# Windowed attention with sink keys: each 128-row block's key band stored as two 64-row halves of 224 columns

## The chip, the cores and the metric

One core of a Trainium2 chip runs the kernel. The metric is the device time of one execution in microseconds (us); the time before is the median of three runs.

## What is computed

Attention with a sliding window of 128 keys and 4 sink keys, for 2 batches of 8 heads, 768 positions and head size 64, in float32. Its output, 768 x 512 for each batch, goes through two blocks of matrix products (a low-rank token mix and a channel network of width 2048; then a token network of width 256 and a channel network of width 1536). Only the attention is touched here:

```
keep   = (key < 4) | ((row - key >= 0) & (row - key < 128))
scores = where(keep, (q @ k.T) / 8, -1e9)
a      = softmax(scores);  out = a @ v
```

So a block of 128 rows needs its own 128 keys, the 128 keys before them, and the first few keys (the sinks). Both limits (4 and 128) are inputs; the masks leave room for up to 32 sinks.

## The kernel before

TensorE (PE) does all products, VectorE (DVE) takes scores out of PSUM, ScalarE (ACT) takes exponentials, GpSimd (POOL) does small steps, and SyncE (SP) issues every DMA. PE and SP run in the order in which the program writes them; the order on DVE, ACT and POOL is the compiler's.

**Attention** (`band_attention`, L296 to L351). The work is 16 units: a batch, a pair of heads, and a half of the rows (half 0 has the blocks i = 0, 1, 2; half 1 has i = 3, 4, 5). A unit has three steps, one for each block, so there are 48 steps t. A step passes three slots; after each slot the planner (`weave`) may put in side work.

- Slot 1, `band_scores` (L197): for each of the two heads e one product of the 64 x 128 queries with 288 columns: 128 keys before, 32 sinks, 128 own keys. Block 0 has only its own 128. Head 0 uses array rows 0 to 63 and head 1 rows 64 to 127; each writes a PSUM bank of its own (0 and 1). Then `band_soft`: DVE adds the mask and takes the minimum of the negated scores (L209), and ACT takes the exponential and the row sum (L213). The result `pr` is stored with the two heads alternating along the columns.
- Slot 2, two steps later, `band_turn`: PE transposes for each head the 128 columns before (L230) and the own 128 (L231; L233 in block 0), and once for both heads the sink columns (L238, from block 2 on). `band_keep` copies them out of PSUM (L247, on ACT for the first block of a unit, on DVE otherwise), and at the end of a unit copies the transposed sinks (L250).
- Slot 3, four steps later, `band_values` (L266): products with the values, in two parts; a block of values serves the own keys of one row block and the keys before of the next in one product of 256 columns, or 128 where there is only one of them. Each head writes 64 of the 128 output rows. Then one product for the sinks of both heads (L272), a copy out (L277), three transposes back (L282), and the division by the row sums (L289, L290).

**Loads.** SP loads a unit's queries and keys at once (`band_load`, L170: 384 query columns and 448 or 608 key columns, two units ahead), the values of a head pair in half 0 (L179), and the sink values (L180).

**Side work.** `weave` (L670) gives each slot a grant of time for PE, DVE, ACT and POOL (`SPREAD`: 0.3, 0.3, 0.3, 0.4 us while fewer than 8 units are finished, then 0.7, 0.6, 0.6, 0.7), adds it to what is left over (at most 1.5), and lets two side lists take steps whose costs are written at their `yield`. A `yield` with a fifth number holds its side for that many slots. The first list (`FEEDS`) decodes weights: `decode_steps` (L423) loads a piece of 512 float64 values for each partition, and turns them into two float32 parts by ACT and POOL (L434, L435), three steps on DVE (L437, L439, L441), and ACT and POOL again (L443, L444). The second (`FILLS`) has the token mix (`mix_down`, `mix_up`) and three "narrow" channel passes c0, c1, c2 (`channel_pass`: products `hp` at L124, ACT and DVE at L623 and L624, products `accs` at L643); c0 starts when the low-rank weights and four weight tiles are decoded. `drain` runs what is left when the attention has been written out.

**After the attention** (from about 188 us) the channel passes of full width run, PE products from end to end (`layers`).

Of the kernel before, what the change touches and what calls it, by code (L numbers as in the profile page):

```python
# [20 lines left out]
P = 128  # L21
# [6 lines left out]
KW = P + SINK  # L28
BAND = P + KW
K0 = 3 * P + 2 * SINK  # L30
K1 = 4 * P + 3 * SINK
MASKED = -8.0e9
FAR = 1.0e30
ATTENTION = {"sc": (0, 1), "tp": (3,), "tsink": (5,), "ot": (6,), "xp": (6,), "tall": (2,), "mix": (4, 7), "acc": (2, 7), "hid": (4,)}
# [8 lines left out]
CHUNK, HOLD = 4, 3  # L43
WARM = 3
# [31 lines left out]
class Net:  # L76
# [4 lines left out]
    def preload(self, x):  # L81
# [4 lines left out]
        n = HALF + K0  # L86
        self.early = flat[:, NS * P:NS * P + n]
        nc.sync.dma_start(self.early, self.ins["qk"][0, 0, 0, :, :n])
        self.ident = c.tile([P, P], F32, name="ident")
        make_identity(nc, self.ident)  # L90
        key, rel, self.span, self.sink = flat[:, :P], flat[:, P:2 * P], flat[:, 2 * P:2 * P + BAND], flat[:, 2 * P + BAND:3 * P + BAND]
        self.key = key
        nc.gpsimd.iota(rel, pattern=[[-1, P]], base=0, channel_multiplier=1, allow_small_or_imprecise_dtypes=True)
        nc.gpsimd.iota(key, pattern=[[1, P]], base=0, channel_multiplier=0, allow_small_or_imprecise_dtypes=True)
        nc.gpsimd.memset(self.span[:, P:KW], 0.0)
        nc.gpsimd.tensor_scalar(self.span[:, :P], rel, float(P), None, ALU.add)
        nc.gpsimd.tensor_scalar(self.span[:, KW:], rel, 0.0, FAR, ALU.is_lt, ALU.mult)
        nc.gpsimd.tensor_tensor(self.span[:, KW:], self.span[:, KW:], rel, ALU.add)
# [45 lines left out]
    def band_masks(self):  # L144
        nc, c = self.nc, self.one
        m0 = c.tile([P, P], F32, name="m0")
        m1 = c.tile([P, BAND], F32, name="m1")
        m2 = c.tile([P, BAND], F32, name="m2")

        def put(out, place, bound):  # L150
            nc.vector.tensor_scalar(out, place, bound, MASKED, ALU.is_ge, ALU.mult)

        put(self.sink, self.key, self.n_sink)
        put(m2, self.span, self.window)
        nc.vector.tensor_tensor(m0, m2[:, KW:], self.sink, ALU.max)
        nc.vector.tensor_tensor(m1[:, 0:P], m2[:, 0:P], self.sink, ALU.max)
        nc.vector.memset(m1[:, P:KW], MASKED)
        put(m1[:, KW:], self.span[:, KW:], self.window)
        put(m2[:, P:KW], self.key[:, 0:SINK], self.n_sink)
        self.masks = [m0, m1] + [m2] * (NS - 2)  # L160

    def band_load(self, unit, ld):
        nc = self.nc
        b, hp, half = unit
        nk = K1 if half else K0
        if unit == (0, 0, 0):
            raw = self.early
        else:
            raw = ld.tile([P, HALF + K1], F32, tag="qk", name="qk", bufs=3)
            nc.sync.dma_start(raw[:, :HALF + nk], self.ins["qk"][b, hp, half, :, :HALF + nk])  # L170
        return {"unit": unit, "raw": raw}

    def band_load_values(self, st, ld):
        nc = self.nc
        b, hp, half = st["unit"]
        if half == 0:
            self.v = ld.tile([P, NS, P], F32, tag="v", name="v")
            self.vs = ld.tile([P, 2 * D], F32, tag="vs", name="vs")
            nc.sync.dma_start(self.v, self.ins["v"][b, hp])  # L179
            nc.sync.dma_start(self.vs, self.ins["vs"][b, hp])  # L180
        st["v"], st["vs"] = self.v, self.vs
# [5 lines left out]
    def band_scores(self, st, ii):  # L187
        nc = self.nc
        half = st["unit"][2]
        i = 3 * half + ii  # L190
        n = BAND if i else P
        k0 = HALF + (ii if half else max(ii - 1, 0)) * KW
        st["sc", ii] = []
        for e in range(2):
            sc = self.bank("sc", "sc")[:, :n]
            head = st["raw"][e * D:(e + 1) * D]
            nc.tensor.matmul(sc, lhsT=head[:, blk(ii)], rhs=head[:, k0:k0 + n], start=True, stop=True)  # L197
            st["sc", ii].append(sc)

    def band_soft(self, st, ii, e, sb):  # L200
        nc = self.nc
        nb, den = st["nb"], st["den"]
        i = 3 * st["unit"][2] + ii
        n = BAND if i else P
        if e == 0:
            st["pr", ii] = sb.tile([P, BAND, 2], F32, tag="pr", name="pr", bufs=3)
        pr = st["pr", ii]
        sm = sb.tile([P, BAND], F32, tag="sm", name="sm", bufs=3)
        nc.vector.tensor_tensor_reduce(  # L209
            sm[:, :n], st["sc", ii][e], self.masks[i][:, :n], scale=-0.125, scalar=3.0e38,  # L210
            op0=ALU.add, op1=ALU.min, accum_out=nb[:, ii, e:e + 1],
        )
        nc.scalar.activation(  # L213
            pr[:, :n, e], sm[:, :n], AF.Exp, bias=nb[:, ii, e:e + 1], scale=-1.0,
            accum_out=den[:, ii, e:e + 1],
        )

    def band_turn(self, st, ii, e):
        nc = self.nc
        half = st["unit"][2]  # L220
        i = 3 * half + ii
        if ii == 0 and e == 0:
            st["pt"] = self.sb.tile([P, 2, 3 * 2 * P], F32, tag="pt", name="pt")
            st["pts"] = self.sb.tile([P, HALF], F32, tag="pts", name="pts")
        pr, pt = st["pr", ii], st["pt"]
        if e == 0:
            st["tp"] = self.bank("tp", "tp").rearrange("p (e k) -> p e k", e=2)
        tp = st["tp"]
        if i > 0:
            nc.tensor.transpose(tp[:, e, 0:P], pr[:, 0:P, e], self.ident)  # L230
            nc.tensor.transpose(tp[:, e, P:], pr[:, KW:, e], self.ident)  # L231
        else:
            nc.tensor.transpose(tp[:, e, P:], pr[:, 0:P, e], self.ident)  # L233
        first = 0 if half else 2
        if ii == first and e == 1:
            st["tsink"] = self.bank("tsink", "tsink")
        if i >= 2 and e == 1:
            nc.tensor.transpose(st["tsink"][:, blk(ii)], pr[:, P:P + D, :].rearrange("p s e -> p (s e)"), self.ident)  # L238

    def band_keep(self, st, ii):  # L240
        nc = self.nc
        half = st["unit"][2]
        pt, tp = st["pt"], st["tp"]
        first = 0 if half else 2
        lo = 0 if 3 * half + ii else P
        copy = nc.scalar.copy if ii == 0 else nc.vector.tensor_copy
        copy(pt[:, :, ii * 2 * P + lo:(ii + 1) * 2 * P], tp[:, :, lo:])  # L247
        if ii == 2:
            s0 = first * P
# [3 lines left out]
    def band_values(self, st, part):  # L253
        nc = self.nc
        half = st["unit"][2]
        pt, pts, v, vs = st["pt"], st["pts"], st["v"], st["vs"]
        if half == 0:
            sinks, steps = (2 * P, 1), [[(0, 0, 2, P)], [(1, P, 2, 3 * P), (2, 2 * P, 1, 5 * P)]]
        else:
            sinks, steps = (0, 3), [[(2, 0, 1, 0), (3, 0, 2, P)], [(4, P, 2, 3 * P), (5, 2 * P, 1, 5 * P)]]  # L260
        if part == 0:
            st["ot"] = self.bank("ot", "ot")
        ot = st["ot"]
        for n, (j, c0, w, p0) in enumerate(steps[part]):
            for e in range(2):
                nc.tensor.matmul(  # L266
                    ot[e * D:(e + 1) * D, c0:c0 + w * P], lhsT=v[:, j, e * D:(e + 1) * D], rhs=pt[:, e, p0:p0 + w * P],
# [635 lines left out]
```

## Time and profile before

| | us |
|---|---|
| median of 3 runs (672.05 to 675.17) | 673.8 |
| the profiled execution | 675.64 |
| its span, first to last instruction | 673.9 |
| PE busy | 655.1 |
| DVE busy | 380.1 |
| ACT busy | 233.1 |
| POOL busy | 187.7 |

"Busy" on PE counts products in flight, also while the next one waits for its weights or for the array to empty, so a busy PE is not PE at its peak. The granted clock is a share of full speed: 1.0 is 2.4 GHz and 0.5 is 1.2 GHz, the two levels that occur. The step times named below are starts of the first DVE step (L209) of a step t.

### The profile page before, as it was taken

Reading aid. Unit: us, or ns where it says so; the run is one execution under the profiler, and the core shown is the slowest. Engines: PE = TensorE matmul, PEld = TensorE weight load, DVE = VectorE, ACT = ScalarE, POOL = GpSimd, SP = SyncE. Lnnn points to the kernel's source line nnn. Section 1 sums busy time; section 2 is a strip of 40 time slices with the busy share of each in tenths; the row PEclk is TensorE's granted clock in tenths of the full one; section 3 lists DMA queues with packets and bytes.
Section 4 is the critical chain, followed back from the end, with each engine's and each line's share of the span. In section 5 each row is a group of like instructions: output and inputs, shape, how many; then the busy total and the mean of one; then the engine's idle time right before and its main releaser. Section 6 shows DMA issues by size and latency. Waiting matters only on the chain.

```text
span 673.9 us, 10189 instructions
## 1 busy us (share of the span) xinstructions
PE 655.1 (97%) x3958; PEld 601.1 (89%) x3958; DVE 380.1 (56%) x790; ACT 233.1 (35%) x568; POOL 187.7 (28%) x205
## 2 busy tenths in 40 slices
PE   8999998998999999999999999999999999999996
PEld 3565666786899999999999999999999999999996
DVE  4868794497354157888872345786241377422223
ACT  4756673355141133433321133532131243211110
POOL 1434562043010044544430022751040254200000
PEclk8999998998999999999999999999999999999999
DMA  4424541422000013434340010322000032000112
GB/s 138 146 80 147 208 146 54 147 100 94 1 1 0 1 46 112 139 116 127 130 146 1 1 63 8 119 94 94 1 1 0 1 125 95 2 0 1 48 48 98
DMA packets 16474, 48.53 MB, mean 72 GB/s; under 512 B 1952, under 2 KB 5152, under 8 KB 16416
## 3 DMA queue, kind: packets, MB, share of 16 engines
q1 hardware_dynamic: 16416, 47.79, 21.4%
q8 instruction: 33, 0.54, 0.3%
q14 instruction: 25, 0.20, 0.1%
HBM read 44.63 MB, written 3.15 MB: 71 GB/s over the span
## 4 chain that ended last, share of the span: by engine, by line
PE 88%; DVE 8%; issue 2%; ACT 1%; POOL 0%; DVEq 0%; ACTq 0%
PE hp L124 34%; PE accs L643 34%; PE sc L197 4%; PE gp L124 3%; PE ot L266 3%; PE up L124 2%; DVE c L439 1%; DVE sm L209 1%; PE tp L230 1%; PE tp L231 1%; DVE c L441 1%; DVE pt L247 1%; PE ot L272 1%; PE tp L124 1%; PE xtp L124 1%
## 5 line engine op out<-in xcount | busy, mean ns | idle before, releaser
L124 PE MATMUL hp<-uh,wh 128*128 128x384 f32 (+1 forms) x464 | 156.4, 337 | 6.1 <-DVE hl L624 6.1
L624 DVE SCALAR_TENSOR_TENSOR hl<-hp,hh 128x384 fp32r<-128x384 f32 (+1 forms) x116 | 62.8, 542 | 176.0 <-ACT hh L623 175.5
L124 PE MATMUL hp<-uh,wl 128*128 128x384 f32 (+1 forms) x464 | 154.1, 332 | 0.0
L643 PE MATMUL accs<-hh,wh 128*128 128x384 f32 (+1 forms) x464 | 154.1, 334 | 0.0
L124 PE MATMUL hp<-ul,wh 128*128 128x384 f32 (+1 forms) x464 | 153.9, 332 | 0.0
L643 PE MATMUL accs<-hh,wl 128*128 128x384 f32 (+1 forms) x464 | 151.9, 330 | 0.0
L623 ACT ACTIVATE hh<-hp 128x384 fp32r<-128x384 f32 (+1 forms) x116 | 55.6, 480 | 261.2 <-PE hp L124 261.1
L444 POOL TENSOR_TENSOR wl<-c,wh 128x512 fp32r<-128x512 f32 x56 | 75.7, 1355 | 172.3 <-ACT wh L443 170.0
L643 PE MATMUL accs<-hl,wh 128*128 128x384 f32 (+1 forms) x464 | 97.1, 329 | 0.0
L124 PEld LDWEIGHTS hp<-uh,wh 128*128 128x128 f32 x464 | 87.7, 189 | 9.9 <-DVE hl L624 6.8
L643 PEld LDWEIGHTS accs<-hh,wh 128*128 128x128 f32 x464 | 87.6, 189 | 2.7 <-ACT hh L623 1.5
L124 PEld LDWEIGHTS hp<-ul,wh 128*128 128x128 f32 x464 | 87.8, 189 | 0.1
L124 PEld LDWEIGHTS hp<-uh,wl 128*128 128x128 f32 x464 | 87.7, 189 | 0.0
L643 PEld LDWEIGHTS accs<-hh,wl 128*128 128x128 f32 x464 | 87.7, 189 | 0.0
L643 PEld LDWEIGHTS accs<-hl,wh 128*128 128x128 f32 x464 | 80.3, 188 | 0.0
L435 POOL TENSOR_SCALAR c<-c 128x512 f32<-128x512 f32 (+2 forms) x65 | 47.8, 735 | 77.4 <-ACT c L434 73.9
L651 DVE TENSOR_TENSOR x<-accs,x 128x384 f32<-128x384 f32 (+1 forms) x118 | 58.7, 557 | 16.8 <-PE accs L643 16.8
L213 ACT ACTIVATE pr<-sm,nb 128x288 f32<-128x288 f32 (+1 forms) x96 | 50.7, 533 | 43.1 <-DVE nb L209 42.5
L439 DVE SCALAR_TENSOR_TENSOR c<-raw,c 128x512 int32<-128x512 int32 (+2 forms) x65 | 60.2, 926 | 1.7
L434 ACT ACTIVATE c<-raw 128x512 f32<-128x512 f32 (+2 forms) x65 | 43.1, 664 | 34.0 <-POOL wl L444 23.8
L441 DVE SCALAR_TENSOR_TENSOR c<-raw,c 128x512 int32<-128x512 int32 (+2 forms) x65 | 53.0, 815 | 1.3
L437 DVE TENSOR_SCALAR c<-c 128x512 int32<-128x512 int32 (+2 forms) x65 | 43.4, 667 | 10.7 <-POOL c L435 10.7
(151 smaller groups left out, 752.0 us busy)
## 6 DMA issues: line engine op xcount, KB each, us to landing
raw<-in_w SPq DMA_DIRECT2D x56, 512.0 KB, 3.6
qk<-in_qk SPq DMA_DIRECT2D x8, 496.0 KB, 3.3
v<-in_v SPq DMA_DIRECT2D x8, 384.0 KB, 5.0
raw<-in_t SPq DMA_DIRECT2D x6, 512.0 KB, 3.5
out<-x SPq DMA_DIRECT2D x16, 192.0 KB, 2.0
qk<-in_qk SPq DMA_DIRECT2D x7, 416.0 KB, 3.2
vs<-in_vs SPq DMA_DIRECT2D x8, 64.0 KB, 4.6
raw<-in_V SPq DMA_DIRECT2D x1, 512.0 KB, 5.3
```

The source lines that it names most:

```text
L124: self.nc.tensor.matmul(out, lhsT=w, rhs=x, start=start and i == 0, stop=stop and i == n - 1, **kw)
L213: nc.scalar.activation(pr[:, :n, e], sm[:, :n], AF.Exp, bias=nb[:, ii, e:e + 1], scale=-1.0, accum_out=den[:, ii, e:e + 1],)
L434: nc.scalar.activation(f32(c), f32(high), AF.Abs)
L435: nc.gpsimd.tensor_scalar(f32(c), f32(c), LARGE, SMALL, ALU.min, ALU.max)
L437: nc.vector.tensor_scalar(c, c, 5, 2, ALU.logical_shift_left, ALU.logical_shift_right)
L439: nc.vector.scalar_tensor_tensor(c, high, -0x40000000, c, ALU.bitwise_and, ALU.bitwise_or)
L441: nc.vector.scalar_tensor_tensor(c, low, 29, c, ALU.logical_shift_right, ALU.bitwise_or)
L444: nc.gpsimd.tensor_tensor(lo[:, pp], f32(c), f32(hi[:, pp]), ALU.subtract)
L623: nc.scalar.activation(hh, hp, AF.Relu)
L624: nc.vector.scalar_tensor_tensor(hl, hp, 0.0, f32(hh), ALU.max, ALU.subtract)
L643: self.nc.tensor.matmul(part, lhsT=lhs, rhs=rhs, start=fresh, stop=last and late == 1, skip_group_check=True)
L651: nc.vector.tensor_tensor(oc, a[:, :per * n].rearrange("p (a c) -> p a c", a=per), oc, ALU.add)
```

## The change

- **Scores.** Each step t loads its own 576 columns: 128 queries, then two bands of 224 keys. Rows 0 to 63 of the block see 64 + 32 + 64 + 64 columns (first half of the block before, 32 first keys, first half of its own block, second half of the block before); rows 64 to 127 see the second half of their own block, 32 first keys, and the same two halves. So a step has four products of 64 x 64 x 224 on the quarters of the array (two row halves h, two heads e), in the order h0 e0, h0 e1, h1 e0, h1 e1; block 0 has them too.
- **Masks** have 224 columns; where a sink key would stand twice it is masked once.
- **Transposes.** Four for a step; the columns 0 to 127 carry 96 that are needed, among them the sinks. `pr` is stored head by head.
- **Values.** Three products for each head and block: one with 128 own-or-before keys for 128 rows, and two with 96 keys (64 and the 32 sinks) for 64 rows each. No sink transposes, copies or products (L238, L250, L272 go). Blocks 0 and 1 of a unit go in one slot, block 2 in the next step.
- **Loads.** Per step 288 KB for queries and keys, three steps ahead, into five buffers; per unit 192 KB (`vx`) and 288 KB (`vy`) for values.
- **Decoding** while the attention runs: the load is issued 6 slots ahead, 2 slots pass before the first DVE step and 1 before the last ACT and POOL step, which now has its own `yield`.
- **After the attention** only the first list is drained; what is left of the second goes in front of the channel passes (`rest`). The path for other limits (`full_steps`) reads the new layout; it doesn't run with these inputs.

```diff
-KW = P + SINK
-BAND = P + KW
+HB = P // 2
+YW = HB + SINK
+BAND = YW + P
+QK = P + 2 * BAND
+AHEAD = 3
+DMA_LAG = 6
...
-    def band_load(self, unit, ld):
+    def band_load(self, t, ld):
+        b, hp, i = t // (NP * NS), t // NS % NP, t % NS
+        if t == 0:
+            return self.early
+        raw = ld.tile([P, QK], F32, tag="qk", name="qk", bufs=AHEAD + 2)
+        self.nc.sync.dma_start(raw, self.ins["qk"][b, hp, i])
+        return raw
...
     def band_load_values(self, st, ld):
+        st["vx"] = ld.tile([P, 3, P], F32, tag="vx", name="vx")
+        st["vy"] = ld.tile([YW, 3, 2 * P], F32, tag="vy", name="vy")
+        three = slice(3 * half, 3 * half + 3)
+        self.nc.sync.dma_start(st["vx"], self.ins["vx"][b, hp, three].rearrange("s p c -> p s c"))
+        self.nc.sync.dma_start(st["vy"], self.ins["vy"][b, hp, three].rearrange("s p c -> p s c"))
...
+    def band_scores(self, st, ii, raw):
+        nc = self.nc
+        st["sc", ii] = [self.bank("sc", "sc")[:, :BAND] for _ in range(2)]
+        for h in range(2):
+            for e in range(2):
+                head = raw[e * D:(e + 1) * D]
+                nc.tensor.matmul(
+                    st["sc", ii][e][h * HB:(h + 1) * HB], lhsT=head[:, h * HB:(h + 1) * HB],
+                    rhs=head[:, P + h * BAND:P + (h + 1) * BAND], start=True, stop=True,
+                )
...
-            st["pr", ii] = sb.tile([P, BAND, 2], F32, tag="pr", name="pr", bufs=3)
+            st["pr", ii] = sb.tile([P, 2, BAND], F32, tag="pr", name="pr", bufs=3)
...
+    def band_turn(self, st, ii):
+        tp = st["tp"] = self.bank("tp", "tp").rearrange("p (e k) -> p e k", e=2)
+        for e in range(2):
+            for x, c in enumerate((0, YW)):
+                nc.tensor.transpose(tp[:, e, blk(x)], st["pr", ii][:, e, c:c + P], self.ident)
...
-            nc.scalar.copy(st["pts"][:, s0:], st["tsink"][:, s0:HALF])
...
+    def band_values(self, st, ii):
+        for c0, w, p0, v, c in ((0, P, P, vx, 0), (0, HB, 0, vy, 0), (HB, HB, HB, vy, P)):
+            n = v.shape[0]
             for e in range(2):
                 nc.tensor.matmul(
+                    ot[e * D:(e + 1) * D, ii * P + c0:ii * P + c0 + w],
+                    lhsT=v[:, ii, c + e * D:c + (e + 1) * D], rhs=pt[:n, ii, e, p0:p0 + w],
+                    start=ii == 0 and v is vx, stop=v is vy, skip_group_check=True,
                 )
-        if part == 1:
-            c = slice(sinks[0], sinks[0] + sinks[1] * P)
-            nc.tensor.matmul(ot[:, c], lhsT=vs, rhs=pts[:, c], start=False, stop=True, skip_group_check=True)
...
-                        if ii == 0 and u + 2 < n:
-                            load(u + 2)
+                        load(t + AHEAD)
...
-                        self.band_values(st[u], ii)
+                        for z in ((0, 1), (2,))[ii]:
+                            self.band_values(st[u], z)
...
     def decode_steps(self, hi, lo, src):
+        if self.phase < 2:
+            fetch(0)
+            yield from self.lag(DMA_LAG)
         for p0 in range(0, total, PIECE):
...
             yield 0, 0, 0.6, 0.8
+            if self.phase < 2:
+                fetch(p0 + PIECE)
...
+            yield from self.lag(2)
             yield 0, 0.34, 0, 0
...
-            yield 0, 0.6, 0.52, 1.23
+            yield 0, 0.6, 0, 0
             nc.vector.scalar_tensor_tensor(c, low, 29, c, ALU.logical_shift_right, ALU.bitwise_or)
+            yield from self.lag(1)
+            yield 0, 0, 0.52, 1.23
```

## Rows read from the trace of the kernel before

**Rows 1.** The page: busy time of PE, and the chain of waits by engine.

```profile
PE 655.1 (97%) x3958; PEld 601.1 (89%) x3958; DVE 380.1 (56%) x790; ACT 233.1 (35%) x568; POOL 187.7 (28%) x205
...
PE 88%; DVE 8%; issue 2%; ACT 1%; POOL 0%; DVEq 0%; ACTq 0%
```

**Rows 2.** Stretches: us, busy PE, PEld, DVE, ACT, POOL (x); clock, DMA share, GB/s.

```profile
0.00:7.50 7.50, 5.96 (x10) 2.18 (x10) 2.30 (x11) 1.49 (x2) 2.84 (x13) 1.00 0.49 146
7.50:22.10 14.60, 13.89 (x68) 8.04 (x68) 8.34 (x35) 8.81 (x32) 0.56 (x3) 0.77 0.45 156
22.10:55.60 33.50, 32.71 (x221) 21.52 (x220) 25.59 (x84) 22.43 (x71) 14.47 (x22) 1.00 0.38 118
55.60:100.40 44.80, 42.12 (x262) 26.61 (x261) 39.24 (x107) 32.43 (x95) 25.10 (x28) 0.96 0.47 162
100.40:173.40 73.00, 66.73 (x476) 53.26 (x475) 46.34 (x123) 33.87 (x101) 20.08 (x23) 0.95 0.27 91
173.40:205.00 31.60, 30.95 (x219) 29.22 (x219) 16.28 (x32) 8.60 (x20) 4.05 (x4) 1.00 0.01 1
205.00:674.00 469.00, 462.77 (x2714) 460.31 (x2712) 242.07 (x402) 125.47 (x247) 120.60 (x114) 1.00 0.18 58
```

**Rows 3.** Timeline of PE, steps 17 to 20: start, us, operation, tiles, records.

```profile
52.12 0.87 PE L266 MATMUL ot<-pt,v 128*64 128x256 f32 x8
52.92 0.49 PE L272 MATMUL ot<-pts,vs 128*128 128x128 f32 x2
53.34 0.49 PE L197 MATMUL sc<-qk 64*128 64x128 f32 x4
53.76 0.39 PE L230 MATMUL tp<-ident,pr 128*128 128x128 f32 x1
...
54.45 0.49 PE L282 MATMUL xp<-ident,os__776 128*128 128x128 f32 x3
54.87 0.76 PE L197 MATMUL sc<-qk 64*128 64x288 f32 x4
55.55 0.39 PE L230 MATMUL tp<-ident,pr 128*128 128x128 f32 x1
55.77 0.28 PE L231 MATMUL tp<-ident,pr 128*128 128x128 f32 x1
55.90 0.28 PE L230 MATMUL tp<-ident,pr 128*128 128x128 f32 x1
56.02 0.28 PE L231 MATMUL tp<-ident,pr 128*128 128x128 f32 x1
...
59.06 0.91 PE L272 MATMUL ot<-pts,vs 128*128 128x384 f32 x2
59.90 1.06 PE L197 MATMUL sc<-qk 64*128 64x288 f32 x4
60.91 0.39 PE L230 MATMUL tp<-ident,pr 128*128 128x128 f32 x1
```

**Rows 4.** DVE groups from 0 to 206 us, shapes apart.

```profile
L209 DVE CUSTOM_DVE_ANT_0 sm<-sc,m 128x288 f32<-128x288 f32 x80 | 34.1, 450 | 13.2 <-PE sc L197 12.8
...
L439 DVE SCALAR_TENSOR_TENSOR c<-raw,c 128x512 int32<-128x512 int32 x15 | 14.8, 984 | 0.2
...
L209 DVE CUSTOM_DVE_ANT_0 sm<-sc,m 128x128 f32<-128x128 f32 x16 | 4.0, 286 | 2.7 <-PE sc L197 2.7
```

**Rows 5.** Waits from 7.5 to 205 us: total, times, longest.

```profile
PEld sc L197 <- DVE nb L209: 7.4, 15, 1.8
...
PE hp L124 <- DVE hl L624: 6.1, 3, 2.4
```

**Rows 6.** One wait of PE, the same columns as rows 2.

```profile
161.00:167.30 6.30, 3.91 (x22) 3.45 (x22) 2.75 (x6) 1.80 (x7) 0.41 (x1) 0.73 0.27 83
```

**Rows 7.** DMA from 0 to 190 us: queue total; loads with us to landing.

```profile
q1 hardware_dynamic: 7632, 21.04, 33.0%
...
qk<-in_qk SPq DMA_DIRECT2D x8, 496.0 KB, 3.3
```

More of the change, by code (lines that the diff above doesn't have):

```diff
@@ L157, in band_masks @@
-        nc.vector.memset(m1[:, P:KW], MASKED)
-        put(m1[:, KW:], self.span[:, KW:], self.window)
-        put(m2[:, P:KW], self.key[:, 0:SINK], self.n_sink)
-        self.masks = [m0, m1] + [m2] * (NS - 2)
-    def band_load(self, unit, ld):
[L163 to L171, printed above, removed]
+        m0, m1, m2 = [c.tile([P, BAND], F32, name=f"m{i}") for i in range(3)]
@@ new lines, in put @@
+        def put(out, place, bound, op=ALU.is_ge):
+            nc.vector.tensor_scalar(out, place, bound, MASKED, op, ALU.mult)
+        own, sink = slice(YW, YW + HB), slice(HB, YW)
+        nc.vector.memset(m0, MASKED)
+        put(m0[:, own], self.key[:, :HB], self.n_sink)
+        put(m2, self.span, self.window)
+        put(m2[:, sink], self.key[:, :SINK], self.n_sink)
+        nc.vector.tensor_tensor(m0[:, own], m2[:, own], m0[:, own], ALU.max)
+        nc.vector.tensor_copy(m0[HB:, :HB], m2[HB:, :HB])
@@ new lines, in band_masks @@
+        nc.vector.tensor_copy(m1, m2)
+        put(m1[:, sink], self.span[:, sink], self.window, ALU.is_lt)
+        nc.vector.tensor_tensor(m1[:, sink], m1[:, sink], m2[:, sink], ALU.min)
+        self.masks = [m0, m1] + [m2] * (NS - 2)
+    def band_load(self, t, ld):
[5 more added lines that the diff above has]
+        return raw
@@ L213, in band_soft @@
         nc.scalar.activation(
-            pr[:, :n, e], sm[:, :n], AF.Exp, bias=nb[:, ii, e:e + 1], scale=-1.0,
-            accum_out=den[:, ii, e:e + 1],
+            st["pr", ii][:, e], sm, AF.Exp, bias=nb[:, ii, e:e + 1], scale=-1.0, accum_out=den[:, ii, e:e + 1],
         )
-    def band_turn(self, st, ii, e):
+    def band_turn(self, st, ii):
         nc = self.nc
[L220 to L238, printed above, removed]
@@ L245, in band_keep @@
[L245 removed]
         copy = nc.scalar.copy if ii == 0 else nc.vector.tensor_copy
[L247 removed]
+        copy(st["pt"][:, ii], st["tp"])
         if ii == 2:
[L249 to L250 removed]
             nc.gpsimd.tensor_scalar_add(st["den"], st["den"], 1.0e-9)
[L253 removed]
+    def band_values(self, st, ii):
         nc = self.nc
[L255 to L261, printed above, removed]
+        pt, vx, vy = st["pt"], st["vx"], st["vy"]
+        if ii == 0:
@@ L543, in mix_up @@
         nc = self.nc
+        while (b, d) not in self.low:
+            yield "wait"
         t = self.low[b, d]
@@ L712, in weave, with drain, left_of, rest @@
                     side["cost"] = next(side["gen"], None)
-    def drain(self, first=0):
-        for side in self.sides[first:]:
-            if side["cost"] is not None:
-                for _ in side["gen"]:
-                    pass
-            for _, f, a in side["todo"]:
-                for _ in f(*a):
-                    pass
-        del self.sides[first:]
+    def drain(self, first=0, last=0):
+        end = len(self.sides) - last
+        for side in self.sides[first:end]:
+            for _ in self.left_of(side):
+                pass
+        del self.sides[first:end]
+    def left_of(self, side):
+        if side["cost"] is not None:
+            yield from side["gen"]
+        for _, f, a in side["todo"]:
+            yield from f(*a)
+    def rest(self, side, main):
+        for cost in self.left_of(side):
+            if cost[0] != "after" and cost[0]:
+                yield cost
+        yield from main
     def add_side(self, todo):
@@ L811, in whole @@
             attention(xs)
+            self.drain(last=1)
+            left = self.sides.pop()
             self.phase = 2
```

154 lines of the change are left out of this document (67 added, 87 removed).

## The prediction

> **What bounds the kernel now.** I read the page's totals and its chain of waits first: PE is busy 97% of the span and carries 88% of the chain, DVE 8% [rows 1]. Then the span by stretches [rows 2]. From 205 us on nothing that the change touches runs, and PE is full there (462.8 of 469.0 us); those 469 us should stay. So the question is the first 205 us. There no engine is the bound all along. In steps 7 to 18 (22.1 to 55.6) and steps 33 to 47 (100.4 to 173.4) PE is the fullest, with DVE at 25.6 of 33.5 and 46.3 of 73.0. In steps 19 to 32 (55.6 to 100.4) DVE is nearly full, 39.2 of 44.8, since four weight tiles are decoded there. After step 47 PE is full again.
>
> Busy PE is not streaming PE, so I take PE's price from starts in the timeline [rows 3], as the distance from a group's first record to the next group's. A score pair of 288 columns takes 55.55 - 54.87 = 0.68 us, one of 128 takes 0.42, the sink product with 384 columns 59.90 - 59.06 = 0.84, and a value group with 256 + 128 columns 52.92 - 52.12 = 0.80. All four fit one rule: N/600 us for N columns (float32, full clock), plus 0.20 with 128 weight columns and 0.16 with 64, for the first weight load and for the emptying before the next group. Two heads cost no more than one: they run side by side, both where they are apart by rows (scores) and where they are apart by output columns (values). A transpose comes every 0.12 us (55.77, 55.90, 56.02), against about 0.11 for those out of a tile stored without gaps (three and the switch to scores in 54.87 - 54.45 = 0.42, so (0.42 - 0.10)/3).
>
> **The change part by part, on PE.**
> - Scores: 0.16 + 224/600 = 0.53, and 0.02 for two more products to start: 0.55, if all four quarters run side by side. No row shows four. Bounds: 0.55, and 0.16 + 2 x 224/600 = 0.91 if they run two by two, 0.36 more. I take 0.55, since each of the two ways of being apart is shown by a row. A step with 288 columns before saves 0.13; block 0 of a sequence (0.42 before) costs 0.13 more.
> - Sinks: the product goes, 0.84 in half 1 and 0.42 in half 0, where it has 128 columns [rows 3]. Sink transposes go: three of 0.12 in half 1, one in half 0; block 0 gets two more of the others. All transposes read without gaps: 12 x 0.01 = 0.12 for a unit.
> - Values: before, half 1 has two groups of 384 columns, 1.60, and half 0 one of 256 and one of 384, 0.59 + 0.80 = 1.39. After, a block has 128 + 64 + 64 = 256 columns for each head: 0.16 + 512/600 = 1.01 for two blocks, 0.59 for one, 1.60 in all. Nothing saved in half 1, 0.21 lost in half 0. Each pass of a 64-column product streams 64/1200 = 0.05 us, while 64 weight columns cost 0.20 - 0.16 = 0.04; if these loads didn't hide behind the streaming, the 12 of a unit would add 0.5. I take none, since the loads of the same size don't show in the value groups of now beyond the first.
>
> Half 1: 3 x 0.13 + 0.84 + 0.36 + 0.12 = 1.71. Half 0: 0.26 - 0.13 + 0.42 - 0.12 - 0.21 + 0.12 = 0.34. A pair of units saves 2.05, eight pairs **16.4 us of PE**.
>
> **On DVE.** L209 takes 0.450 us for 288 columns and 0.286 for 128 [rows 4], 1.03 ns a column, so 0.384 for 224: 80 x 0.066 - 16 x 0.098 = 3.7 us less. The PSUM copies that go (sinks) were ACT's, which is far from full (33.9 of 73.0 us, [rows 2]), so they are worth nothing.
>
> **The decoding** moves. I count slots by the costs and grants of the planner: each piece takes 3 slots more, and each tile 6 more for its load. The four tiles w0 to w3, whose decoding ended in step 32, end in step 37; c0 starts in step 37 instead of 33, c2 in step 49 instead of 46. So steps 19 to 32 lose a tile, six DVE steps of at most 0.98 [rows 4], up to 5.9 us, beside 14/48 of 3.7 us; that is more than the 14/48 of 16.4 = 4.8 us that PE gives back there, and so DVE can follow. The price is at the end: all of c2 now runs when the attention has almost nothing left to put between its products. Each narrow pass began with a wait of PE for `hl` (three waits, 6.1 us, [rows 5]), and the last brought half a clock window's loss: 0.27 x 6.3 = 1.7 us [rows 6]. Between one more such wait with its clock (2.4 + 1.7) and nothing I take +2.
>
> **A new wait.** The order h0 e0, h0 e1, h1 e0, h1 e1 on PE means that head 0 is complete only after head 1's bank is free; before, its 288 columns were ready for DVE while head 1 waited (59.90 to 60.91 is such a pair, 1.01 instead of 0.68, [rows 3]). PE's weight load for scores waited 15 times for DVE [rows 5]. Each of those can now cost DVE the scores' 0.55 us, 8.3 in all, if no copy or decoding step is there to fill it, or nothing; I take +1.5, since DVE's own idle time for scores was 12.8 us over 80 calls [rows 4], little of it for want of other work. Behind PE's wait stand the transposes of step t-2 and its side work, which in steps 33 to 47 is what PE would run anyway.
>
> **The loads.** 48 x 288 KB and 16 x 480 KB, 22.0 MB, replace 11.1 MB. The queue moved 21.0 MB in 190 us at 33.0% [rows 7]; 32 MB are 50% by bytes, somewhat more for shorter runs. The load comes three steps ahead and lands in 3.3 us [rows 7]; three steps are at least 3 x 1.8 us. SP waits for its five buffers in order, and what stands behind is later loads. I take nothing; without that cover the first seven steps could lose up to 3 us. Mask building has some small steps more, under the products that warm PE up before 7.5 us: nothing, at most 1.
>
> **Sum:** -16.4 + 2 + 1.5 = -12.9. The profiled execution took 675.64, its span and 1.7 us around it, and stands 1.8 above the median of the runs shown. 675.6 - 12.9 = 662.7, which on the median's scale is **661**.
>
> **Rivals.**
> 1. *DVE stays the bound where it is now*, steps 19 to 32 and the seven steps 39 to 45 where w4 and w5 are decoded. For it: 39.2 of 44.8. Against: in 22.1 to 55.6 and 100.4 to 173.4 DVE has 20% to 35% free [rows 2], and the slots spread the decoding. PE's saving is lost in 21 of 48 steps (7.2) and DVE gives back 21/48 of 3.7 (1.6): 661 + 7.2 - 1.6 = **666.6**. The Trainium skill states this as a rule (TensorEngine Tiling, PSUM Bottleneck: tiling speeds up TensorE and not the reading of PSUM, which may become the bottleneck); by it the sum would be this rival's, and the trace bears it out in one stretch of three.
> 2. *The wait for head 1's bank costs its full price*, 8.3 instead of 1.5, and two further half-clock windows at 1.7 follow from the idle PE: 661 + 6.8 + 3.4 = **671**, hardly a change. For it: 15 waits. Against: DVE mostly has other work.
> 3. *Slower: the quarters run two by two*, that is, the change doesn't get what its products are laid out for. 48 x 0.36 = 17.3 us in the score steps: 661 + 17.3 = **678**. It decides from a distance of 12.9/48 = 0.27 us between the first and the second pair; above that the gain is gone. Against: pairs by rows and pairs by columns each run side by side [rows 3]. For: no row has both at once. The Trainium skill lists 64 x 64 as four independent tiles (TensorEngine Tiling, Tiling Modes); no run here shows it yet.
>
> **How the numbers follow.** A measurement of this kernel can tell about 0.5%, 3.4 us, from no change, so faster means below 670.4 and slower above 677.2. Forecast 0.52 (its own range 650 to 666), rival 1 0.22, rival 2 0.12, rival 3 0.11, the rest 0.03. The low end: PE's waits for scores (7.4, [rows 5]) go, and neither the tail's 2 nor the bank's 1.5 is paid: 661 - 10.9 = 650. The high end holds rival 2's 671 and a late load on top, 672; rival 3 is left out. Faster: forecast, rival 1 and a little of rival 2, 0.76; slower: rival 3 and some mishap, 0.12; the same 0.12.
>
> **What would show it.** Scores: four products with starts some 0.01 us apart and 0.55 us to the next group; at 0.9, rival 3. No records of L238 and L272, and the time from the last value group of a unit to the next scores only the switch. DVE's share: if steps 19 to 32 keep 44.8 us with DVE above 39, rival 1. PE's wait for DVE before scores: about as now (7.4 us) or up by 7, rival 2. c2 behind the last scores, with its wait for `hl`. PE from the start of the full-width passes unchanged at about 469 us. I am wrong if the attention shortens by less than 9 us with quarters side by side, or if the 469 us move.

## The result, and the profile after

The changed kernel takes 682.5 us (median of 4 runs, 680.4 to 683.88) beside 674.47 for the kernel before on the same chip (4 runs, 672.05 to 675.17). The ratio is 1.0123, with an interval of 1.0085 to 1.0161: slower, by more than the 0.5% that can be told from no change. The forecast was 661.0 with a range up to 672, so both the sign and the range were wrong. The profiled execution took 680.4 us, its span 678.6.

The page after: busy time by engine, and the chain of waits by engine. PE's busy time fell by 16.0 us against [rows 1], and the span grew by 4.7.

```profile
PE 639.1 (94%) x4454; PEld 597.6 (88%) x4454; DVE 373.1 (55%) x792; ACT 226.7 (33%) x552; POOL 184.9 (27%) x208
...
PE 83%; DMA 6%; DVE 4%; ACT 4%; issue 2%; POOL 0%; SPq 0%; DVEq 0%; ACTq 0%; POOLq 0%
```

DMA stands in the chain with 6%, and was not there at all before. The stretches after (columns as in [rows 2]; the last border is set at 209.7 instead of 205.0, where PE runs products of full width from end to end):

```profile
0.00:7.40 7.40, 5.78 (x14) 2.08 (x14) 2.54 (x12) 1.49 (x2) 3.58 (x16) 1.00 0.46 127
7.40:22.50 15.10, 9.51 (x100) 5.54 (x100) 7.42 (x33) 7.86 (x28) 2.23 (x7) 0.91 0.89 265
22.50:66.50 44.00, 32.74 (x338) 22.53 (x339) 27.05 (x88) 21.59 (x71) 12.05 (x18) 0.81 0.57 174
66.50:115.30 48.80, 39.83 (x433) 28.93 (x432) 34.43 (x104) 30.32 (x89) 22.02 (x27) 0.92 0.60 188
115.30:175.80 60.50, 55.34 (x586) 45.81 (x587) 43.78 (x125) 30.30 (x93) 18.52 (x23) 1.00 0.56 172
175.80:209.70 33.90, 33.63 (x267) 32.82 (x266) 15.01 (x30) 9.71 (x24) 5.82 (x6) 1.00 0.00 1
209.70:678.60 468.90, 462.31 (x2721) 459.87 (x2719) 242.92 (x405) 125.44 (x247) 120.72 (x114) 1.00 0.18 58
```

The last stretch is 468.9 us, as before. Its border is chosen and is no event of the program, since the first products of full width run earlier, between the last ones of the attention. An event that both kernels have says the same: the first product into `accs` with 384 columns, before and after.

```profile
192.59 0.34 PE L643 MATMUL accs<-hh,wh 128*128 128x384 f32 x1
```

```profile
198.46 0.35 PE L635 MATMUL accs<-hh,wh 128*128 128x384 f32 x1
```

From there to the end are 481.3 us before and 480.1 after. So everything happens ahead of it, and two more answers of the view of stretches, one row for all of it, keep the account. The kernel before, 205.0 us:

```profile
0.00:205.00 205.00, 192.36 (x1246) 140.83 (x1247) 138.08 (x389) 107.62 (x321) 67.09 (x91) 0.96 0.31 104
```

The changed kernel, 209.7 us:

```profile
0.00:209.70 209.70, 176.83 (x1735) 137.72 (x1736) 130.23 (x388) 101.27 (x305) 64.22 (x94) 0.93 0.50 154
```

PE is busy 15.5 us less, close to what was forecast, but it is idle 32.9 us instead of 12.6. In steps 6 to 18 alone (22.5 to 66.5, 44.0 us; before they ran from 20.3 to 55.6) PE is busy in 32.7 of 44.0 us, at a granted clock of 0.81; no engine is full there. Where the idle time comes from, the waits of the changed kernel from 7.4 to 206 us say (total, times, longest):

```profile
ACT c L421 <- DMA raw<-in_w: 21.7, 9, 4.1
PEld sc L191 <- DVE nb L202: 20.1, 15, 6.7
PE sc L191 <- DVE nb L202: 16.6, 8, 6.6
...
DVE c L425 <- POOL c L422: 14.5, 5, 4.2
...
PE xtp L126 <- DVE t L529: 7.3, 2, 3.9
...
ACT c L421 <- DMA raw<-in_V: 4.8, 2, 3.2
```

Another row adds 3.2 us for `raw<-in_U`, so ACT stood 29.7 us in front of the first decoding step for weights that hadn't landed. The same view of the kernel before has 9.9:

```profile
ACT c L434 <- DMA raw<-in_w: 8.9, 4, 3.5
...
ACT c L434 <- DMA raw<-in_V: 1.0, 2, 0.7
```

One step shows how that reaches PE. Step 10 lasts from 32.31 to 41.58 us, 9.3 us; its neighbours take 1.7 and 2.4. The timeline of ACT in it (start, us, line, operation, idle time before):

```profile
31.59 0.47 ACT L206 ACTIVATE pr<-sm,nb 128x224 f32<-128x224 f32 x1
31.96 0.19 ACT L206 ACTIVATION_READ_ACCUMULATOR pr<-sm,nb 128x1 f32 x1
35.33 0.66 ACT L421 ACTIVATE c<-raw 128x512 f32<-128x512 f32 x1 [3.19 <-DMA raw<-in_V]
35.90 0.50 ACT L510 CAST xh<-x 128x384 fp32r<-128x384 f32 x1
36.30 0.48 ACT L206 ACTIVATE pr<-sm,nb 128x224 f32<-128x224 f32 x1
...
38.99 0.44 ACT L421 ACTIVATE c<-raw 128x256 f32<-128x256 f32 x1 [1.66 <-DMA raw<-in_V]
```

and that of DVE:

```profile
32.61 0.39 DVE L202 CUSTOM_DVE_ANT_0 sm<-sc,m 128x224 f32<-128x224 f32 x1
32.92 0.08 DVE L202 DVE_READ_ACCUMULATOR2_ANT nb<- 128x1 f32 x1
32.92 0.68 DVE L222 COPY pt<-tp 128x512 f32<-128x512 f32 x1
36.72 1.20 DVE L425 TENSOR_SCALAR c<-c 128x512 int32<-128x512 int32 x1 [3.12 <-POOL c L422]
...
39.95 0.29 DVE L425 TENSOR_SCALAR c<-c 128x256 int32<-128x256 int32 x1 [0.57 <-POOL c L422]
40.28 1.38 DVE L427 SCALAR_TENSOR_TENSOR c<-raw,c 128x256 int32<-128x256 int32 x1
41.58 0.38 DVE L202 CUSTOM_DVE_ANT_0 sm<-sc,m 128x224 f32<-128x224 f32 x1
```

And that of PE, whose row before this one begins at 35.02:

```profile
42.02 1.33 PE L191 MATMUL sc<-qk 64*64 64x224 f32 x8 [6.60 <-DVE nb L202]
```

The exponentials of step 10 had their input at 32.7 and 33.0 us (L202) and started at 36.30, because L421 stands ahead of them on ACT and waited for a load that was issued at 30.05 and landed at 35.31. On DVE the steps of two pieces stand between L202 of step 10 and L202 of step 11, whose scores PE had begun at 33.62: it started at 41.58. PE waited for it 6.60 us with the scores of step 12 (42.02), and these then took 1.33 us instead of 0.61: the granted clock had fallen to 0.5, the lower level. Steps 4, 16, 26 and 31 (6.8, 8.0, 6.0 and 7.8 us) are of the same kind, each with a wait of ACT for a load of 2.5 to 3.6 us in it.

The delay reaches PE by the side work too. At 91.66 and 108.45 us PE waits 3.9 and 3.4 us before products of the token mix (`xtp`, 7.3 us in the rows above). Their input `t` comes from an ACT step (L528) that stands behind L421, which had waited 3.6 and 3.0 us for its load.

The load itself is not slower than before: the 512 KB pieces landed after 5.2 us (median) in both kernels. What is new is where their first user stands on ACT.

### The profile page after: what moved, and what is told of

Same layout as the page of the kernel before. It is cut to its first block, busy times and chain, and to the rows that moved or that the text cites. A ratio compares the mean times of both kernels' runs of the same rounds, so it can differ in the third digit from the quotient of the medians.

```text
span 678.6 us, 11341 instructions
## 1 busy us (share of the span) xinstructions
PE 639.1 (94%) x4454; PEld 597.6 (88%) x4454; DVE 373.1 (55%) x792; ACT 226.7 (33%) x552; POOL 184.9 (27%) x208
## 4 chain that ended last, share of the span: by engine, by line
PE 83%; DMA 6%; DVE 4%; ACT 4%; issue 2%; POOL 0%; SPq 0%; DVEq 0%; ACTq 0%; POOLq 0%
PE accs L635 34%; PE hp L126 34%; DMA raw<-in_w 4%; PE gp L126 3%; PE tp L217 2%; PE sc L191 2%; PE ot L235 2%; PE up L126 2%; ACT pr L206 2%; DMA raw<-in_V 1%; PE tp L126 1%; DVE c L427 1%; PE xtp L126 1%; PE xp L569 1%; PE w L112 1%
## 5 line engine op out<-in xcount | busy, mean ns | idle before, releaser
L126 PE MATMUL hp<-uh,wh 128*128 128x384 f32 (+1 forms) x464 | 154.4, 333 | 3.3 <-DVE hl L616 3.3
L434 POOL TENSOR_TENSOR wl<-c,wh 128x512 fp32r<-128x512 f32 x56 | 76.5, 1369 | 178.9 <-ACT wh L433 176.6
L422 POOL TENSOR_SCALAR c<-c 128x512 f32<-128x512 f32 (+2 forms) x65 | 45.8, 705 | 102.6 <-ACT c L421 98.1
L421 ACT ACTIVATE c<-raw 128x512 f32<-128x512 f32 (+2 forms) x65 | 43.1, 663 | 56.1 <-POOL wl L434 25.6
L427 DVE SCALAR_TENSOR_TENSOR c<-raw,c 128x512 int32<-128x512 int32 (+2 forms) x65 | 57.0, 877 | 1.9
L206 ACT ACTIVATE pr<-sm,nb 128x224 f32<-128x224 f32 x96 | 45.5, 475 | 33.7 <-DVE nb L202 33.2
L425 DVE TENSOR_SCALAR c<-c 128x512 int32<-128x512 int32 (+2 forms) x65 | 42.0, 647 | 24.2 <-POOL c L422 24.2
L429 DVE SCALAR_TENSOR_TENSOR c<-raw,c 128x512 int32<-128x512 int32 (+2 forms) x65 | 53.8, 828 | 1.4
```

The source lines that it names most:

```text
L126: self.nc.tensor.matmul(out, lhsT=w, rhs=x, start=start and i == 0, stop=stop and i == n - 1, **kw)
L206: nc.scalar.activation(st["pr", ii][:, e], sm, AF.Exp, bias=nb[:, ii, e:e + 1], scale=-1.0, accum_out=den[:, ii, e:e + 1],)
L421: nc.scalar.activation(f32(c), f32(high), AF.Abs)
L422: nc.gpsimd.tensor_scalar(f32(c), f32(c), LARGE, SMALL, ALU.min, ALU.max)
L425: nc.vector.tensor_scalar(c, c, 5, 2, ALU.logical_shift_left, ALU.logical_shift_right)
L427: nc.vector.scalar_tensor_tensor(c, high, -0x40000000, c, ALU.bitwise_and, ALU.bitwise_or)
```

## The experiments

All ratios are to the kernel before, run beside them on the same chip. The first question was which part of the change brings the wait: the new slots of the decoding, the new attention, its larger loads, or the order that the compiler gave to ACT and DVE.

**The changed attention with the old decoding (`e1_old_decode`).** The edit puts back the kernel before's `decode_steps`:

```diff
-        if self.phase < 2:
-            fetch(0)
-            yield from self.lag(DMA_LAG)
...
-            yield from self.lag(2)
...
-            yield from self.lag(1)
```

> The changed attention with the decoding of before (load at the piece's own slot, no lags). Theory order: ACT and DVE still take decode steps ahead of the softmax before their load has landed, so ACT still waits some 20 us for decode loads in the first 180 us and the time stays at 675 to 690 us. Rival volume: nothing changes either, 680 to 685 us. Rival decode (the new slots of the decoding are what costs): the attention's saving appears, 658 to 668 us, and ACT's wait for decode loads falls to the 9 us of before.

Measured: 684.27 us (676.82 to 685.19), ratio 1.0108 (1.0046 to 1.017). ACT's wait for the loads is still there (19.6 us for w, 4.6 for U, 1.6 for V), and so is PE's for DVE before scores (14.4 and 12.1). The new slots don't cause the loss.

```profile
ACT c L403 <- DMA raw<-in_w: 19.6, 9, 3.8
```

**The old attention with the changed decoding (`e2_new_decode`).** The same lines, added to the kernel before.

> The attention and loads of before with the changed decoding alone (load 6 slots ahead, lags). Theory order: loads of half the size and issued a unit ahead, so decode loads are late about as often as before: 668 to 676 us. Rival volume: the same, 670 to 676 us. Rival decode: it costs what the change costs, 680 to 686 us, with ACT waiting 20 us or more for decode loads.

Measured: 666.3 us (665.31 to 667.29), ratio 0.9872 (0.9848 to 0.9896). That is less than the 668 to 676 that were expected. ACT waits 4.7 us for loads:

```profile
ACT c L453 <- DMA raw<-in_w: 4.0, 3, 1.5
...
ACT c L453 <- DMA raw<-in_V: 0.7, 2, 0.5
```

So the changed decoding by itself is worth 8 us, where I had counted 2 us against it; the clock, 0.95 and 0.96 in places before, is 1.00 from 22.5 us on, and PE's wait for `hl` is 2.7 us instead of 6.1 [rows 5].

**Less to load (`e4_thin_loads`).** Both row halves read the first 224 key columns and the first half of `vy`, and the rest is not loaded:

```diff
-        self.nc.sync.dma_start(raw, self.ins["qk"][b, hp, i])
+        self.nc.sync.dma_start(raw[:, :P + BAND], self.ins["qk"][b, hp, i, :, :P + BAND])
...
-        st["vy"] = ld.tile([YW, 3, 2 * P], F32, tag="vy", name="vy")
+        st["vy"] = ld.tile([YW, 3, P], F32, tag="vy", name="vy")
```

> The changed kernel with 352 of 576 columns loaded for queries and keys and half of each vy, which leaves out the second half's own keys and values (both row halves use the first band); the same number of DMAs and PE products. 16.2 MB instead of 24 MB... of it the attention's own loads fall from 22.0 to about 14 MB. Rival volume: most of the loss goes, 660 to 670 us, and the decode loads land in under 4 us. Theory order: decode loads are still issued too late for the place that their steps have on ACT, 676 to 683 us, with waits of 15 us or more for them.

Measured: 678.65 us (676.13 to 680.22), ratio 1.0068 (1.0042 to 1.0093). ACT still waits 21.3 + 4.0 + 1.4 us for the weights. PE's own waits before scores fall (6.0 us instead of 16.6), but those before the token mix rise (11.7 instead of 7.3), and each of these four follows an L421 that had waited for its load:

```profile
PE xtp L126 <- DVE t L529: 11.7, 4, 4.7
...
PE sc L191 <- DVE nb L202: 6.0, 7, 2.0
```

So which product of PE pays depends on what stands behind the waiting step. The volume of the loads is worth some 4 us at most (the intervals of the two ratios overlap) and not the loss.

**The other engines in program order too (`e5_program_order`).** DVE, ACT and POOL then run in the order written, as PE does:

```diff
-            with tc.manual_schedule(engines=MANUAL | ORDERED):
+            with tc.manual_schedule(engines=MANUAL | ORDERED | REST):
```

> The changed kernel with DVE, ACT and POOL also in the order of the program during the attention, so that the lags of the decoding hold; nothing else is changed. Theory order: ACT's wait for decode loads falls below 5 us, PE's wait for DVE before scores from 20 to 10 us or less, no step of the attention over 6 us without fill work, and the time is 655 to 668 us. Rival volume and rival decode: the loads land as late as now and the time stays at 678 to 690 us.

Measured: 686.57 us (685.27 to 687.23), ratio 1.0171 (1.0149 to 1.0193). The waits for the weights are gone altogether, and step 19 begins at 50.9 us instead of 66.5. But the time expected was missed: the written order has waits of its own (ACT for `nb` 56.1 us, POOL for `wh` 39.7), and from 66.5 to 115.3 PE is busy in only 38.2 of 48.8 us. That the loads' wait comes from the order is shown; that the written order is a cure is refuted.

**Only the first decoding step held back (`e6_pin_decode`).** If the order is the cause, moving one instruction of each piece must be enough. L421 is queued on ACT behind the last exponential that the program wrote before it; all else in the program is the changed kernel, and the compiler orders the rest anew:

```diff
-        nc.scalar.activation(
+        self.exp = nc.scalar.activation(
...
-            nc.scalar.activation(f32(c), f32(high), AF.Abs)
+            if self.phase < 2 and self.exp is not None:
+                with self.tc.issue_after(self.exp.ins):
+                    nc.scalar.activation(f32(c), f32(high), AF.Abs)
```

> The changed kernel; during the attention each decode piece's first ACT step is queued behind the last exponential written before it, so that the slots between load and use hold on ACT, while everything else keeps the scheduler's order. Theory order (decode steps stand ahead of the softmax on ACT and DVE before their load has landed): ACT's wait for decode loads falls from 30 us to under 8, PE's wait for DVE before scores from 36 to under 15, the granted clock rises to 0.985 or more, time 656 to 670 us. Rival (the attention's own loads or its own order cost the time): 677 us or more.

Measured: **654.19 us** (653.87 to 656.11), ratio 0.9728 (0.9672 to 0.9785), the best version of the study, 28 us below the changed kernel. No wait of ACT for a load is left. The waits of PE before scores from 7.4 to 206 us, and the attention with the narrow passes in one row, up to 185 us:

```profile
PEld sc L191 <- DVE nb L202: 8.3, 17, 1.7
...
PE sc L191 <- DVE nb L202: 4.4, 6, 1.5
```

```profile
0.00:185.00 185.00, 170.05 (x1741) 133.58 (x1742) 128.51 (x391) 101.07 (x305) 64.31 (x94) 0.99 0.57 174
```

Step 10 takes 2.1 us. The loads are the same ones, at a higher rate (174 GB/s against 154) and with nearly the same landing (4.9 us median for a piece of w, 5.2 in the changed kernel). The 17 pieces decoded in the attention now land 2 to 17 us before their first ACT step takes them; in the changed kernel 12 of 17 landed after ACT had come to them. The first DVE steps of V stand in step 13 instead of step 10. What follows the 185 us takes 467.7 us.

The rows also divide the gain. Against the changed kernel's 209.7 us these are 24.7 us less: PE's idle time falls by 17.9 us (32.9 to 14.95), and its busy time by 6.8 us (176.8 to 170.05) at a granted clock of 0.99 instead of 0.93.

**The old attention with the changed decoding, held back in the same way (`e9_before_pin`),** so that the layout can be read without the wait:

> The attention and loads of before with the changed decoding and the same queueing of each piece's first ACT step. Theory order: there only 6 us of waiting for decode loads were left with the changed decoding alone (666 us), so 660 to 667 us, a few us slower than the changed kernel with the queueing. Rival (the old attention is the better one): faster than that by 5 us or more.

Measured: 666.46 us (665.02 to 674.54, 10 runs), ratio 0.9905 (0.9866 to 0.9944), no better than `e2_new_decode`: before, there was little to hold back. Its row up to the full-width passes:

```profile
0.00:195.00 195.00, 184.00 (x1248) 137.17 (x1249) 135.48 (x389) 108.46 (x321) 63.51 (x91) 1.00 0.32 109
```

The two last rows differ by the new attention with its loads, at nearly the same clock: PE is busy 14.0 us less (184.00 - 170.05), 3.9 of which come back as idle time (11.0 against 14.95). The medians differ by 12.3 us.

**The old decoding, held back (`e11_pin_old_decode`).** `e1_old_decode` with the edit of `e6_pin_decode`.

> The changed attention with the decoding of before, where a piece's load and its first ACT step have the same slot, and that step queued behind the last exponential before it. Theory order: the queueing alone gives no lead, since nothing lies between load and use, so part of the loss comes back: 663 to 680 us with ACT waiting 10 us or more for decode loads. Rival (the queueing does it all, the changed slots of the decoding are idle): within 3 us of the 654 us of the changed decoding with queueing.

Measured: 664.8 us (663.26 to 665.19), ratio 0.9876 (0.9826 to 0.9926). ACT's waits for loads fall from 25.8 us to 2.1. The time is as expected, the wait isn't: 10 us or more had been expected, since load and use have the same slot. Holding the step back removes it without the new slots. It is worth 19.5 us here by the medians and about 16 by the ratios, as one run of `e1_old_decode` is 7 us faster than its others. The new slots are worth another 10.6 on top (654.19); with them PE's wait for `hl` is 1.8 us instead of 6.6.

**More buffers (`e3_more_buffers`).** In the chain of the changed kernel, SP issues the load of V's second piece only after a `qk` load, which had waited for one of its five buffers; so SP's queue could be the cause.

```diff
-        raw = ld.tile([P, QK], F32, tag="qk", name="qk", bufs=AHEAD + 2)
+        raw = ld.tile([P, QK], F32, tag="qk", name="qk", bufs=AHEAD + 5)
...
+        st["vx"] = ld.tile([P, 3, P], F32, tag="vx", name="vx", bufs=3)
+        st["vy"] = ld.tile([YW, 3, 2 * P], F32, tag="vy", name="vy", bufs=3)
```

> The changed kernel with eight instead of five buffers for queries and keys and three instead of two for the values, so that SP is held back less by PE's progress; no queueing of decode steps. Rival SP (decode loads are late because SP issues them behind key loads that wait for a buffer): with three more steps of room they land in time, 655 to 665 us. Theory order: the scheduler, which knows of the buffers, puts the decode steps earlier on ACT and DVE by as much, ACT waits 15 us or more for decode loads and the time is 673 to 686 us.

Measured: 681.05 us (678.72 to 683.54), ratio 1.0131 (1.0071 to 1.0191). ACT's waits for loads come to 26.7 us (17.6 + 6.1 + 3.0), PE's to 16.1 and 12.8. With the buffers V's first load was issued at 20.6 us instead of 30.0, but the compiler also moved V's decoding steps about three steps earlier on DVE; the wait went along. More room for SP doesn't remove the wait. As the order moved with it, the run doesn't show what SP's queue alone is worth.

**The two attentions alone (`e7_alone_after`, `e8_alone_before`).** All weights are asked for only after the attention in the program (the rest of these two kernels can't be compared with the others):

```diff
-FEEDS = ((1, "V"), (5, "w"), (7, "w"), (8, "w"), (9, "w"), (12, "w"), (13, "w"))
+FEEDS = ((17, "V"), (17, "w"), (17, "w"), (17, "w"), (17, "w"), (17, "w"), (17, "w"))
```

> The changed kernel with no decoding (so no side work either) during the attention; it all comes after it, so that the whole takes far longer and only the attention's steps 6 to 47 are read. Theory: free of decode loads the changed steps run at 1.8 to 2.0 us, 74 to 82 us for 41 steps. Rival loads (459 KB a step don't come fast enough, or SP's order holds them back): 2.2 us or more a step, over 90 us, with PE or DVE waiting for qk, vx or vy.

> The same for the kernel before. Theory: 2.1 to 2.3 us a step, 86 to 94 us for the 41 steps, about 12 us more than the changed attention. Rival loads: as fast as the changed one or faster.

In the changed kernel the edit doesn't do what it was meant for. The trace has the first weight load at 7.6 us, and U, V and 14 pieces of w are decoded beside steps 3 to 19. Steps 6 to 47 take 114.3 us, where 74 to 82 were expected; from 35 to 83 us DVE is busy in 45.4 of 48.0 us, at a granted clock of 0.57. The kernel before has its first weight load at 88.6 us, near the end of its attention, and takes 90.3 us for the same steps, within the 86 to 94 expected. So only places where both have nothing beside the attention can be compared: steps 20 to 39 of the changed one and the pair from 62.08 us of the other.

A unit takes 6.13 us after (96.26 to 102.39, the scores of one place in a unit to those of the next), a pair 12.26; before, a pair takes 13.00 (62.08 to 75.08). The gain is 0.74 us a pair, not the 2.05 forecast, and a step takes 2.04 us, not the 1.8 to 2.0 expected. The timeline of PE in the changed one alone shows where the rest is:

```profile
96.26 0.61 PE L191 MATMUL sc<-qk 64*64 64x224 f32 x8
97.30 0.66 PE L217 MATMUL tp<-ident,pr 128*128 128x128 f32 x4 [0.43 <-ACT pt L222]
97.80 0.55 PE L249 MATMUL xp<-ident,os__1058 128*128 128x128 f32 x3
98.28 0.74 PE L191 MATMUL sc<-qk 64*64 64x224 f32 x8
99.02 0.66 PE L217 MATMUL tp<-ident,pr 128*128 128x128 f32 x4
...
102.39 0.61 PE L191 MATMUL sc<-qk 64*64 64x224 f32 x8
```

Once in a unit the transposes wait 0.43 us until ACT has emptied their only bank, and once the scores take 0.74 instead of 0.54: the records of that group start at 98.277 and then at 98.418, 98.425 and 98.431, the second head's bank having come free late. That is 1.26 us a pair, and 0.74 + 1.26 = 2.0 (2.1 if the first wait is taken from starts too, 1.04 instead of 0.54): the products got cheaper as forecast, and PE, with nothing else to do, waits. Two more kernels ask whether these waits count beside the side work.

**A second bank for the transposes (`e10_two_tp`),** on top of `e6_pin_decode`:

```diff
-ATTENTION = {"sc": (0, 1), "tp": (3,), "ot": (6,), "xp": (6,), "tall": (2,), "mix": (4, 7), "acc": (2, 7), "hid": (4,)}
+ATTENTION = {"sc": (0, 1), "tp": (3, 5), "ot": (6,), "xp": (6,), "tall": (2,), "mix": (4, 7), "acc": (2, 7), "hid": (4,)}
```

> The changed kernel with the queueing and two PSUM banks for the transposes, the second being the one that the sink transposes left free. In the attention alone (2.04 us a step) PE's transposes waited for the copy of the step before out of their one bank, 18 us for ACT and 8 us for DVE over 100 us. If that wait counts, 648 to 653 us; if side work fills it, 653 to 656 us.

Measured: 655.85 us (655.72 to 655.98), ratio 0.9747 (0.97 to 0.9794): no gain. The wait changes its name (PE's weight load for transposes now waits 7.6 us for `pr`, 3.6 without the bank). The Trainium skill advises to rotate independent products through different banks (Perfetto Trace Analysis, Matmuls). `e7_alone_after` shows the wait that this would save, and here saving it gave nothing. That side work already fills it is the likely reason and not shown: from 22.5 to 66.5 us the granted clock is 0.88 instead of 0.96, and a gain of a few us could lie under that.

**Head by head (`e12_head_order`),** also on top of `e6_pin_decode`: the order h0 e0, h1 e0, h0 e1, h1 e1, so that the first head need not wait for the second bank.

```diff
-        for h in range(2):
-            for e in range(2):
+        for e in range(2):
+            for h in range(2):
```

> The changed kernel with the queueing and the four score products in the order h0 e0, h1 e0, h0 e1, h1 e1, so that head 0 doesn't wait for head 1's bank. If the bank wait that was predicted costs anything it shows here: 650 to 653 us and PE's wait for DVE before scores below 8 us; if it is hidden, 653 to 656 us. If the quarters need the other order to run side by side, 660 us or more.

Measured: 659.22 us, ratio 0.9778 (0.9703 to 0.9853); two runs at 655.2 and 655.5, two at 663.0. PE's waits before scores fall a little (the weight loads' 7.2 from 8.3, the products' 2.4 from 4.4), and nothing is gained. The four products still run side by side (a group takes 61.88 - 61.34 = 0.54 us, and in 35 of 48 steps all four start within 0.03 us, 33 in `e6_pin_decode`), so the order of the quarters is not what makes this long run long. The profiled run is one of the long ones, with a clock of 0.88 to 0.95 in three stretches where `e6_pin_decode` has 0.96 to 1.00; why it falls there was not followed further.

## Why the prediction was wrong, point by point

- **The prices of the products: right.** A score group takes 34.16 - 33.62 = 0.54 us, forecast 0.55, and the first records of its four products start at 33.622, 33.628, 33.635 and 33.642:

```profile
33.62 0.61 PE L191 MATMUL sc<-qk 64*64 64x224 f32 x8
34.16 0.66 PE L217 MATMUL tp<-ident,pr 128*128 128x128 f32 x4
34.75 0.44 PE L235 MATMUL ot<-pt,vx 128*64 128x128 f32 x4
35.02 0.40 PE L235 MATMUL ot<-pt,vy 96*64 96x64 f32 x8
```

  Rival 3, quarters two by two, falls. The Trainium skill's four independent tiles of 64 x 64 (TensorEngine Tiling (Array Packing), Tiling Modes) agree with these 7 ns. The sink steps are gone. Three value blocks took 1.65 us (99.61 to 100.66 and 101.79 to 102.39 in `e7_alone_after`), forecast 1.60.
- **The sum for PE, 16.4 us: nearly right.** The same layout measured 14.0 us of busy time (`e9_before_pin` against `e6_pin_decode`), and 12.3 us of the median against the -16.4 + 1.5 = -14.9 that the sum has for it. Both come from runs with the first decoding step held back; without that the new attention is slower with either decoding.
- **The bank wait, +1.5: right in kind.** Its price is 0.2 us once a unit where nothing fills it, 3.2 in all, and removing it gained nothing (`e12_head_order`: 655.2 and 655.5 us in the two runs at a granted clock of 0.997, as in `e6_pin_decode`). The other bank wait, 0.43 us a unit before the transposes, has no term in the sum. Rival 2 is not what happened: the long waits of PE before scores (up to 6.7 us) are for an L202 that stood behind decoding on DVE, and go with `e6_pin_decode`.
- **DVE as the bound, rival 1: no.** From 66.5 to 115.3 us DVE is busy in 34.4 of 48.8 us, less than before. L202 takes 0.385 us, as forecast (0.384). In `e6_pin_decode` DVE has 39.1 of those 48.8 and PE 43.8. The Trainium skill's sentence that the copy out of PSUM may become the bottleneck (TensorEngine Tiling (Array Packing), PSUM Bottleneck) is not borne out by these two rows.
- **The full-width passes unchanged, 469: right** (480.1 us from the first product into `accs` with 384 columns, 481.3 before).
- **The tail of the decoding, +2: wrong in sign.** The new slots are worth -8 (`e2_new_decode`) to -10.6 (`e11_pin_old_decode` to `e6_pin_decode`). The pass c2 does begin behind the last scores (175.8 and 171.3 us in the changed kernel), but its wait for `hl` didn't come: PE waits 3.3 us for `hl`, the last time at 155.3, and products of the first full-width pass (from 178.5) run between those of c2.
- **The step that failed** is "the loads ... I take nothing", with "the slots spread the decoding" behind it. I counted the slots as if every engine kept to them, and priced only whether `qk` lands in time. It does; no product waits for it. But the slots bind PE and SP. The first user of a weight load is on ACT, whose order is the compiler's, and with the new attention its step came to stand ahead of exponentials that were ready, in front of a load with up to 4 us still to go. ACT stood 29.7 us instead of 9.9, DVE's next decoding steps held L202 up behind them, PE's weight loads waited 20.1 us before scores instead of 7.4 [rows 5], and the granted clock up to the full-width passes was 0.93 instead of 0.96. The volume is some 4 us of it at most (`e4_thin_loads`); more buffers and the old slots took none of it away (`e3_more_buffers`, `e1_old_decode`).
- **The range** was wrong for the same reason: no rival had this wait. Rival 3's 678 lies nearest to the measured time by chance, since its mechanism is not there. The sign of this wait was in the view that [rows 5] come from: the 8.9 us of L434 for `raw<-in_w`, in four waits of up to 3.5, stood above both rows that I took, and I passed over it as ACT is far from full. [Rows 7] gave the landing of `qk` (3.3 us) and not that of the weights (5.2).

With the loads' wait out of the way the sum would have been beaten: 654.19 against 661. But that comes from two errors of opposite sign: the layout gave 12.3 us for 14.9, and the decoding took 8 to 10.6 us away, where the sum adds 2. What stays open is why the compiler sets the first decoding step so much earlier beside the new attention; its order is seen in the traces, its reasons are not.

## What to carry to other kernels

Before you price a change by slots or lags, ask for each engine whose order it is: a step that waits for a DMA on an engine that the compiler orders can come to stand ahead of work that is ready, and here every engine behind it paid. In the table of waits read the rows of idle engines too where what they wait for is a DMA, since such an engine still hands work on. Then hold that one step back behind the work it must not delay, and not whole engines in their written order: 654.19 us against 686.57.

## What the runs showed that was not expected

- The new decoding gains 8 us beside the old attention, and the new layout 12.3 us once the first decoding step is held back. The kernel with both and without that hold is 8 us slower.
- Three engines in the order written removed the wait in question and lost more elsewhere: `e5_program_order` reached step 19 at 50.9 us, 4.7 ahead of the kernel before (55.6), and ended 12 us behind it.
- In `e7_alone_after` decoding that the program writes behind the attention ran beside its first twenty steps, so what the compiler orders can move far.
- Alone, PE's steps after the change are 2.04 us (6.13 for three) and before 2.17 (13.00 for six): with nothing to put between its products, 1.26 of the 2.0 us by which a pair's products got cheaper go into waits for a bank.
